# Weight conversion in an attention and MoE kernel: a sign joined from two inputs, or written as two 16-bit halves

## The chip, the cores and the metric

The kernel runs on one core of a Trainium2 chip. A core has five engines that run side by side, each with its own queue of instructions that it takes strictly in order: TensorE (PE, with its weight load PEld), VectorE (DVE), ScalarE (ACT), GpSimd (POOL) and SyncE (SP), which here issues every DMA. Results go from engine to engine through the on-chip memory SBUF and, out of TensorE, through PSUM. The metric is the time of one execution on the device, in microseconds, as the median of the runs.

## The reference: what is computed

```python
q_d = q.reshape(B, H, Sd, factor, D).mean(axis=3)     # factor 4; k_d, v_d likewise
out_up = np.repeat(sm_attn(q_d, k_d, v_d), factor, axis=2)
mask = np.abs(pos[:, None] - pos[None, :]) < factor
scores = np.where(mask, scale * (q @ k.T), -1e9)
out_local = softmax(scores) @ v
x = (out_up + out_local)      # 8 batches x 576 tokens, 512 wide
h = x @ w_in                  # 512 x 2048
g = np.maximum(0.01 * h, h)
out = g @ w_out               # 2048 x 512
```

Attention has 8 batches, 8 heads, 576 positions and a head width of 64. Its two parts, one over positions averaged by four and one over a band of seven positions, are added. Then come two dense layers over 4608 tokens. The weights w_in and w_out arrive as float64, the rest as float32.

## The kernel before

**Weights.** TensorE multiplies float32 in a rounded format (float32r). To keep precision the kernel splits every weight into a rounded part (tiles wih, woh) and the remainder (wil, wol), does the same with the activations (xh, xl; gh, gl), and adds three products for each block: high by high, high by low, low by high (L638 for the first layer, L678 for the second).

The weights must first be made from float64. One tile is 128 x 512 numbers; there are 16 of w_in and 16 of w_out, so `convert(f, k)` runs 32 times. A float64 lies in memory as two 32-bit words, the low word first. The tile `st` is seen as words: `low` is every other word from the first, `top` every other from the second. The steps are:

1. SP loads the tile (helper `load`, L181) into a staging buffer. There are seven of these, lent by other uses of the same memory: k, v, two of prod, up and, for the first few, xh1 and xl1. In the profile the tiles have these names.
2. ACT (L226) turns the low word into an integer from 0 to 7: the three bits that a float32 keeps of it, rounded. It is written over the low word.
3. DVE (L228) takes the sign bit of the top word and joins it into that integer. This is a scalar_tensor_tensor with two inputs, top and low.
4. ACT (L231) takes the absolute value of the top word, read as float32, and scales it by 2 to the power -112, so that its exponent is that of a float32.
5. DVE (L233) shifts the top word left by 3 and joins the integer of step 3 into it: now it is the float32.
6. ACT (L239) rounds it into wih or woh.
7. POOL (L241) subtracts the rounded part and writes the remainder into wil or wol. Then the staging buffer is free for another load.

**Attention.** Batch 0 is done by TensorE in bands of 64 positions (`banded`: scores L405 and L413, softmax, transposes L440, values L458 with windows of v that are loaded as su_vw). Its averaged part is `pooled` (averages by POOL L293, L295 or DVE L299, scores L312, softmax, transposes L351, values L363). The other batches' bands are done by POOL (products L507, L562) and DVE (sums L513, L568).

**Passes.** The dense layers run over half batches of 256 or 320 tokens. The first two half batches go twice, over the first eight blocks of the inner width and later over the other eight; all others go once over the 16 blocks.

**The order.** Nothing is scheduled by the compiler. Every piece of work is a generator that yields its operations with an estimated length; the class `Order` plays them through, takes at each step the operation that can start first (then the one of lower rank), and writes the instructions out in that order. An operation on an engine is estimated at a fixed part plus a part per element: on ACT 0.13 + 0.00083 n us, on DVE 0.08 + 0.00104 n, on POOL 0.25 + 0.00217 n. SP's loads are put in order in the same way, and each has to wait on the chip until the buffer that it fills is really free. So an estimate decides the place of an instruction, not when it runs.

Of the kernel before, what the change touches and what calls it, by code (L numbers as in the profile page):

```python
# [7 lines left out]
F32R = mybir.dt.float32r  # L8
I32 = mybir.dt.int32
U32 = mybir.dt.uint32  # L10
BF16 = mybir.dt.bfloat16
AF = mybir.ActivationFunctionType
ALU = mybir.AluOpType
# [21 lines left out]
LOW, ROUND = 0.876 * 2.0 ** -29, 0.484375  # L35
# [109 lines left out]
def attn_moe(ctx: ExitStack, tc, qkt, vd, qb, kb, vb0, vb1, vwb, band, identb, w_in, w_out, ident, edge, out):  # L145
    nc = tc.nc
# [11 lines left out]
    def slot(*tags):  # L158
        return (yield ("slot", tags, 0))

    def sb(s, shape, dtype, pool=None):
        tag = s.tag
        return (pool or wk).tile(shape, dtype, name=tag, tag=tag, bufs=bufs[tag])
# [4 lines left out]
    def op(eng, n, *after, times=1):  # L168
        if eng == "PE":
            dur = n  # L170
        else:
            a, k = COST[eng]
            dur = times * a + k * n
        return (yield ("op", eng, dur, max((0.0,) + after), 0, after))
# [4 lines left out]
    def load(out, in_, size, *after):  # L179
        t = yield ("op", "SP", 0.3, max((0.0,) + after), size)  # L180
        nc.sync.dma_start(out=out, in_=in_)  # L181
        return t

    def wait(name, n=1):
        return (yield ("wait", name, n))

    id_sb = const.tile([128, 128], F32, name="id_sb")
    edge_sb = const.tile([128, BLK, W], F32, name="edge_sb")
    band_sb = const.tile([128, S // 64, WIN], BF16, name="band_sb")
    idb_sb = const.tile([128, 128], BF16, name="idb_sb")  # L190
    w_in_v = w_in.rearrange("(c p) (f m) -> p f c m", p=128, m=128 * WORDS)
# [18 lines left out]
    def weight(f, k):  # L210
        f0, *ts = max((w for w in wts if w[0] <= f), key=lambda w: w[0])
        return ts[2 * k][:, f - f0], ts[2 * k + 1][:, f - f0]
# [3 lines left out]
    def convert(f, k):  # L216
        s = yield from slot("k", "v", "prod", "up", *(("xh1", "xl1") if f < 4 else ()))
        st = sb(s, [128, 512, 2], U32)
        if k == 0:
            t = yield from load(st.rearrange("p (c m) w -> p c (m w)", c=NC), w_in_v[:, f], 524e3, s.t)  # L220
        else:
            t = yield from load(st.rearrange("p m w -> p (m w)"), w_out_v[:, f], 524e3, s.t)
        low, top = st[:, :, 0], st[:, :, 1]
        li, ti, tf = low.bitcast(I32), top.bitcast(I32), top.bitcast(F32)
        t = yield from op("ACT", 512, t)
        nc.scalar.activation(out=li, in_=low, func=AF.Copy, scale=LOW, bias=ROUND)  # L226
        t1 = yield from op("DVE", 870, t)
        nc.vector.scalar_tensor_tensor(out=li, in0=ti, scalar=-(1 << 31), in1=li,  # L228
                                       op0=ALU.bitwise_and, op1=ALU.bitwise_or)
        t = yield from op("ACT", 512, t1)  # L230
        nc.scalar.activation(out=tf, in_=tf, func=AF.Abs, scale=REBIAS)  # L231
        t = yield from op("DVE", 870, t)
        nc.vector.scalar_tensor_tensor(out=ti, in0=ti, scalar=3, in1=li,  # L233
                                       op0=ALU.logical_shift_left, op1=ALU.bitwise_or)
        if f >= FSPLIT:
            yield from wait("late")
        hi, lo = (w.rearrange("p c m -> p (c m)") for w in weight(f, k))
        t = yield from op("ACT", 512, t)
        nc.scalar.copy(out=hi, in_=tf)  # L239
        t = yield from op("POOL", 590, t)  # L240
        nc.gpsimd.tensor_tensor(out=lo, in0=tf, in1=hi.bitcast(F32), op=ALU.subtract)  # L241
        s.free(t)
        od.signal(("w", f, k), t)
# [486 lines left out]
    with tc.manual_schedule():  # L730
        od.spawn(0, fixed())
        for b in range(B):
            od.spawn(0, outd_tile(b))
            for hf in range(2):
                od.spawn(0, x_tile(b, hf))
        for c in range(NC):
            od.spawn(1 + c, pooled(0, c, 1 + c, sup))
            od.spawn(1.5 + c, banded(0, c, 0, 1.5 + c, sup))
            od.spawn(26 + 0.1 * c, banded(0, c, 1, 26, sup))
        for f in range(NF):  # L740
            for k in range(2):
                od.spawn((20 if f < HF else 40) + 2 * (f % HF) + k, convert(f, k))
        od.spawn(0, swap())
        od.spawn(0, edges())
        od.spawn(0, opened())
        od.spawn(5000, down_proj())
        od.spawn(4999, up_proj())
        for b in range(BANDED, B):
            for c in range(NC):
                od.spawn(88 + 10 * b + 0.1 * c, pooled(b, c, 0))  # L750
            for hf in range(2):
                for u in range(2):
                    od.spawn(89 + 10 * b + 4 * hf + u, scores(b, hf, u))
                    od.spawn(90 + 10 * b + 4 * hf + u, widen(b, hf, u))
                    od.spawn(90 + 10 * b + 4 * hf + u, values(b, hf, u))
        od.run()
# [60 lines left out]
```

## Time and profile before

| | |
|---|---|
| median of 3 runs | 983.59 us (982.6 to 985.67) |
| the profiled execution, its own time | 980.87 us |
| its span in the profile | 979.1 us |
| mean granted clock of TensorE | 0.983 |
| joins of step 3 (L228) | 32, from 19.9 to 129.3 us of the span |
| first large matmul (L638) | 48.48 us |

The span runs from the first to the last instruction of the trace; the execution's own time has 1.77 us beside it. In the profile L228 is line 228 of the kernel, and 128x512 int32 an operand's partitions, elements and type. "Busy" counts the time from the start to the end of an instruction, so time that it spends held up after it has begun counts too. In lines of groups, idle time stands with the instruction that ended it. Three numbers with slashes are the shortest, the median and the longest duration in ns.

### The profile page before, as it was taken

To read this page: it belongs to the slowest core of one execution; us is meant where nothing else is said; L and a number is where in the kernel's file an instruction comes from. 1 tells how busy PE (TensorE), PEld (TensorE's weight loads), DVE (VectorE), ACT (ScalarE), POOL (GpSimd) and SP (SyncE) were. 2 spreads that over 40 slices of the span, in tenths; PEclk is the share of its full clock that TensorE was granted. 3 is DMA by queue.
4 is the path that set the end of the run, shared out by engine and by line. 5 is a ranking of instruction groups with operands and counts; after the bars stand their busy time and mean duration, and the time that the engine had idled before them with its cause. 6 is when DMAs were issued, how large, how long until landed. Compare 5 with 4: busy or idle time off the path is not lost.

```text
span 979.1 us, 18709 instructions
## 1 busy us (share of the span) xinstructions
PE 948.0 (97%) x7434; PEld 913.0 (93%) x7434; DVE 616.5 (63%) x987; ACT 432.2 (44%) x1251; POOL 613.5 (63%) x362
## 2 busy tenths in 40 slices
PE   5796999999999999999999999999999999999998
PEld 4596999889999999999999999999999999999998
DVE  4997778878866877587665976547563756151111
ACT  4887966444533543255422554234332324242212
POOL 3553467888797878887787878758695777310000
PEclk9597999999999999999999999999999999999999
DMA  9546763624531542225223441304131121000000
GB/s 286 188 148 204 232 223 127 197 99 156 166 108 56 185 136 94 68 92 179 82 89 109 154 147 61 111 4 158 39 108 55 54 71 52 30 23 6 23 1 27
DMA packets 51959, 106.46 MB, mean 109 GB/s; under 512 B 4464, under 2 KB 30320, under 8 KB 51872
## 3 DMA queue, kind: packets, MB, share of 16 engines
q1 hardware_dynamic: 51872, 105.28, 32.9%
q8 instruction: 58, 0.95, 0.4%
q14 instruction: 29, 0.24, 0.1%
HBM read 94.64 MB, written 10.62 MB: 108 GB/s over the span
## 4 chain that ended last, share of the span: by engine, by line
PE 91%; DMA 3%; ACT 2%; issue 1%; DVE 1%; POOL 1%; SPq 0%; POOLq 0%; ACTq 0%
PE hp L638 42%; PE acc L678 40%; PE pt L312 2%; PE pt L363 2%; PE pt L351 2%; DMA su_vw<-in_vwb_dram 1%; PE pt L598 1%; DMA v<-in_w_out_dram 1%; DMA vs<-in_vd_dram 1%; POOL wol L241 0%; POOL wil L241 0%; DVE prod L228 0%; PE pt L413 0%; ACT pd L324 0%; SPq L181 0%
## 5 line engine op out<-in xcount | busy, mean ns | idle before, releaser
L562 POOL TENSOR_TENSOR prod<-v,s 128x896 f32<-128x896 f32 (+1 forms) x112 | 270.1, 2417 | 85.8 <-DVE xloc L568 64.3
L638 PE MATMUL hp<-xh,wih 128*128 128x320 f32 (+1 forms) x1024 | 312.7, 305 | 1.7 <-ACT xh L611 1.3
L678 PE MATMUL acc<-gh,woh 128*128 128x320 f32 (+1 forms) x1024 | 307.9, 301 | 0.5 <-ACT o L713 0.4
L638 PE MATMUL hp<-xl,wih 128*128 128x320 f32 (+1 forms) x1024 | 304.0, 297 | 0.1
L638 PE MATMUL hp<-xh,wil 128*128 128x320 f32 (+1 forms) x1024 | 303.8, 297 | 0.0
L678 PE MATMUL acc<-gh,wol 128*128 128x320 f32 (+1 forms) x1024 | 301.8, 295 | 0.0
L678 PE MATMUL acc<-gl,woh 128*128 128x320 f32 (+1 forms) x1024 | 301.7, 295 | 0.0
L507 POOL TENSOR_TENSOR prod<-q,k 128x896 f32<-128x896 f32 (+1 forms) x112 | 265.1, 2373 | 36.1 <-DMA k<-in_kb_dram 22.9
L648 ACT ACTIVATE gh<-hp 128x320 fp32r<-128x320 f32 (+1 forms) x256 | 105.4, 412 | 364.5 <-PE acc L678 339.6
L651 DVE TENSOR_TENSOR gl<-hp,gh 128x320 fp32r<-128x320 f32 (+1 forms) x256 | 116.2, 455 | 221.4 <-ACT hp L649 220.3
L638 PEld LDWEIGHTS hp<-xh,wih 128*128 128x128 f32 x1024 | 194.6, 190 | 8.6 <-issue 5.5
L678 PEld LDWEIGHTS acc<-gh,woh 128*128 128x128 f32 x1024 | 192.7, 188 | 4.7 <-issue 2.6
L638 PEld LDWEIGHTS hp<-xl,wih 128*128 128x128 f32 x1024 | 195.0, 190 | 0.3 <-DVE xl L613 0.3
L638 PEld LDWEIGHTS hp<-xh,wil 128*128 128x128 f32 x1024 | 194.8, 190 | 0.0
L678 PEld LDWEIGHTS acc<-gl,woh 128*128 128x128 f32 x1024 | 192.7, 188 | 0.0
L678 PEld LDWEIGHTS acc<-gh,wol 128*128 128x128 f32 x1024 | 192.4, 188 | 0.0
L568 DVE TENSOR_REDUCE xloc<-prod 128x128 f32<-128x896 f32 (+1 forms) x112 | 133.9, 1196 | 22.7 <-POOL prod L562 21.4
L513 DVE TENSOR_REDUCE s<-prod 128x14 f32<-128x896 f32 (+1 forms) x112 | 133.4, 1193 | 19.5 <-POOL prod L507 19.1
L649 ACT ACTIVATE hp<-hp 128x320 f32<-128x320 f32 (+1 forms) x256 | 104.0, 406 | 0.0
L605 DVE TENSOR_TENSOR pt<-pt,up 128x256 f32<-128x256 f32 (+1 forms) x56 | 38.7, 709 | 32.3 <-PE pt L598 30.6
L299 DVE TENSOR_REDUCE qk_d<-qk 128x288 f32<-128x1152 f32 x29 | 38.9, 1342 | 11.8 <-DMA qk<-in_qkt_dram 11.7
L324 ACT ACTIVATE pd<-pt,st_d 128x144 f32<-128x144 f32 x84 | 32.0, 381 | 26.8 <-DVE st_d L321 19.5
(119 smaller groups left out, 777.5 us busy)
## 6 DMA issues: line engine op xcount, KB each, us to landing
qk<-in_qkt_dram SPq DMA_DIRECT2D x32, 576.0 KB
k<-in_kb_dram SPq DMA_DIRECT2D x14, 704.0 KB
v<-in_vb_dram SPq DMA_DIRECT2D x14, 704.0 KB
vs<-in_vd_dram SPq DMA_DIRECT2D x32, 288.0 KB
k<-in_kb_dram SPq DMA_DIRECT2D x14, 640.0 KB
v<-in_vb_dram SPq DMA_DIRECT2D x14, 640.0 KB
out_dram<-o SPq DMA_DIRECT2D x36, 160.0 KB
out_dram<-o SPq DMA_DIRECT2D x36, 128.0 KB
```

The lines of the kernel that those rows point to most:

```text
L299: nc.vector.tensor_reduce(out=qk_d, in_=qkr, axis=AX.X, op=ALU.add)
L324: nc.scalar.activation(out=pd[:, qi], in_=scv[:, qi], func=AF.Exp, scale=SCALE / (FAC * FAC), bias=mx[:, qi:qi + 1], accum_out=sm[:, qi:qi ...
L507: nc.gpsimd.tensor_tensor(out=prv, in0=q[:, p, a - j0:z - j0].unsqueeze(2).to_broadcast([128, n, W, D]), in1=view(k[:, p], (a - j0) * D, [ ...
L513: nc.vector.tensor_reduce(out=s[:, p, a - j0:z - j0], in_=prv, axis=AX.X, op=ALU.add)
L562: nc.gpsimd.tensor_tensor(out=prv, in0=view(v[:, p], a - j0, [[1, n], [nv, D], [1, W]]), in1=s[:, p, a - j0:z - j0].unsqueeze(2).to_broadc ...
L568: nc.vector.tensor_reduce(out=xl_t[:, :n, p], in_=prv, axis=AX.X, op=ALU.add)
L605: nc.vector.tensor_tensor(out=xv, in0=xv, in1=upv, op=ALU.add)
L638: nc.tensor.matmul(hp[:, :n], wt[:, c], x[:, c], start=k == 0, stop=k == 3 * NC - 1)
L648: nc.scalar.activation(out=gh[:, :n], in_=hp[:, :n], func=AF.Prelu, alpha=0.01)
L649: nc.scalar.activation(out=hp[:, :n], in_=hp[:, :n], func=AF.Prelu, alpha=0.01)
L651: nc.vector.tensor_tensor(out=gl[:, :n], in0=hp[:, :n], in1=gh[:, :n].bitcast(F32), op=ALU.subtract)
L678: nc.tensor.matmul(acc[:, :n], wt[:, es], g[:, :n], start=f == f0 and j == 0, stop=f == f1 - 1 and j == 2)
```

## The change

The low word, the top word and the float64 are now also seen as 16-bit halves: of the four halves of a number, 0 and 1 are the low word and 3 is the upper half of the top word, which has the sign. ACT writes its integer into half 0 alone. DVE reads half 3, keeps its highest bit and writes that into half 1, by a tensor_scalar with one input. Halves 0 and 1 together are then the word that the join made, and step 5 reads it as before. The estimate for the DVE step goes from 870 to 520 elements.

```diff
+U16 = mybir.dt.uint16
...
         low, top = st[:, :, 0], st[:, :, 1]
+        half = st.rearrange("p m w -> p (m w)").bitcast(U16).rearrange("p (m h) -> p m h", h=4)
         li, ti, tf = low.bitcast(I32), top.bitcast(I32), top.bitcast(F32)
         t = yield from op("ACT", 512, t)
-        nc.scalar.activation(out=li, in_=low, func=AF.Copy, scale=LOW, bias=ROUND)
-        t1 = yield from op("DVE", 870, t)
-        nc.vector.scalar_tensor_tensor(out=li, in0=ti, scalar=-(1 << 31), in1=li,
-                                       op0=ALU.bitwise_and, op1=ALU.bitwise_or)
+        nc.scalar.activation(out=half[:, :, 0], in_=low, func=AF.Copy, scale=LOW, bias=ROUND)
+        t1 = yield from op("DVE", 520, t)
+        nc.vector.tensor_scalar(out=half[:, :, 1], in0=half[:, :, 3], scalar1=0x8000, scalar2=None, op0=ALU.bitwise_and)
```

## The prediction

> **What bounds the kernel now.** I read the page first, for the share of each engine and for the course of the span in 40 slices.
>
> ```profile
> span 979.1 us, 18709 instructions
> PE 948.0 (97%) x7434; PEld 913.0 (93%) x7434; DVE 616.5 (63%) x987; ACT 432.2 (44%) x1251; POOL 613.5 (63%) x362
> ...
> PE   5796999999999999999999999999999999999998
> ...
> PEclk9597999999999999999999999999999999999999
> ```
>
> TensorE is busy for 97%, and what it lacks lies almost all in the first four slices of 24.5 us. So I cut the span into stages, busy time of each engine by stage.
>
> ```profile
> core 0: us, PE busy (x) PEld busy (x) DVE busy (x) ACT busy (x) POOL busy (x), PEclk, DMA share, GB/s
> 0.00:25.00 25.00, 15.09 (x118) 10.29 (x118) 12.09 (x27) 11.67 (x36) 8.96 (x15) 1.00 0.96 287
> 25.00:48.50 23.50, 17.28 (x179) 12.08 (x177) 22.05 (x35) 20.61 (x51) 12.13 (x11) 0.58 0.59 188
> 48.50:75.00 26.50, 26.29 (x270) 24.80 (x269) 24.64 (x47) 22.57 (x57) 14.44 (x11) 0.99 0.49 156
> 75.00:93.00 18.00, 10.27 (x107) 8.48 (x107) 13.79 (x23) 13.19 (x36) 4.91 (x4) 0.83 0.79 247
> 93.00:135.00 42.00, 42.00 (x310) 39.60 (x311) 32.03 (x49) 36.36 (x89) 22.14 (x15) 0.95 0.64 208
> 135.00:979.00 844.00, 837.03 (x6461) 817.73 (x6459) 511.88 (x809) 327.79 (x988) 550.95 (x308) 1.00 0.28 92
> ```
>
> ```profile
> 48.48 0.58 PE L638 MATMUL hp<-xh,wih 128*128 128x256 f32 x1
> ```
>
> Three things stand here. From 135 us on TensorE lacks 844.00 - 837.03 = 6.97 us of 844: the conversions are over, and only a changed order can act there. Between 25 and 48.5 us, before the first large matmul (the row at 48.48), DVE is busy for 94% and ACT for 88%, TensorE waits, at a granted clock of 0.58. Between 75 and 93 us TensorE lacks 18.00 - 10.27 = 7.73 us, at a clock of 0.83. A saving is worth something only where it shortens one of these two stretches; from 93 to 135 us TensorE has no gap, so what is won before is carried on.
>
> What ends the waits, by the list of waits and the chain that ended last:
>
> ```profile
> PE pt L458 <- DMA su_vw<-in_vwb_dram: 5.3, 2, 3.7
> ...
> SPq L181 <- POOL wil L241: 41.9, 13, 9.3
> ...
> 37.73 1.31 POOL wol L241
> ...
> 39.49 4.29 DMA su_vw<-in_vwb_dram
> ...
> 73.37 5.75 DMA su_vw<-in_vwb_dram
> ...
> 85.51 3.93 DMA su_vw<-in_vwb_dram
> ```
>
> Batch 0's banded values (L458) wait for small window loads. These stand in SP's one queue behind weight loads, and a weight load waits until POOL's subtraction (L241) has freed its staging buffer. So the speed of the whole conversion, ACT, DVE, ACT, DVE, ACT, POOL, sets when the windows arrive.
>
> **The join as it runs.** The operation that is replaced, by stage:
>
> ```profile
> core 0: us, DVE busy (x), PEclk, DMA share, GB/s
> 0.00:25.00 25.00, 1.38 (x2) 1.00 0.96 287
> 25.00:48.50 23.50, 7.03 (x7) 0.58 0.59 188
> 48.50:75.00 26.50, 7.59 (x7) 0.99 0.49 156
> 75.00:93.00 18.00, 4.59 (x6) 0.83 0.79 247
> 93.00:135.00 42.00, 8.92 (x10) 0.95 0.64 208
> ```
>
> That is 32 joins and 29.51 us, 0.92 each. Undisturbed one takes 0.68. The rest is seen in the timeline, where the join meets POOL's subtraction:
>
> ```profile
> 28.62 1.30 POOL L241 TENSOR_TENSOR wol<-v,woh 128x512 fp32r<-128x512 f32 x1
> ...
> 28.72 1.75 DVE L228 SCALAR_TENSOR_TENSOR prod<-prod 128x512 int32<-128x512 int32 x1
> ...
> 30.50 0.69 ACT L231 ACTIVATE prod<-prod 128x512 f32<-128x512 f32 x1 [0.39 <-DVE prod L228]
> ...
> 64.04 1.73 POOL L241 TENSOR_TENSOR wil<-k,wih 128x512 fp32r<-128x512 f32 x1 [1.32 <-ACT wih L239]
> ...
> 64.72 1.60 DVE L228 SCALAR_TENSOR_TENSOR prod<-prod 128x512 int32<-128x512 int32 x1
> 66.24 0.51 DVE L420 TENSOR_REDUCE lst<-pt 128x5 f32<-128x350 f32 x1
> ...
> 81.67 1.30 POOL L241 TENSOR_TENSOR wil<-up,wih 128x512 fp32r<-128x512 f32 x1 [2.71 <-ACT wih L239]
> ...
> 82.36 1.16 DVE L228 SCALAR_TENSOR_TENSOR prod<-prod 128x512 int32<-128x512 int32 x1
> ...
> 83.44 1.34 DVE L299 TENSOR_REDUCE qk_d<-qk 128x288 f32<-128x1152 f32 x1
> ```
>
> POOL ends at 29.92, 65.77 and 82.97; the joins end at 30.47, 66.32 and 83.52: each time 0.55 later. A join that begins while the subtraction runs stands still until it is over and then does its whole work.
>
> **The new DVE operation.** It has one input. These rows bound it:
>
> ```profile
> L228 DVE SCALAR_TENSOR_TENSOR k<-k x6: 669/684/1040, 19.9 to 115.9; 128x512 int32<-128x512 int32 x6
> ...
> L299 DVE TENSOR_REDUCE qk_d<-qk x29: 1300/1342/1353, 4.8 to 666.3; 128x288 f32<-128x1152 f32 x29
> ...
> L341 DVE TENSOR_REDUCE v_d<-vs x32: 1184/1206/1218, 14.4 to 672.3; 72x256 f32<-72x1024 f32 x32
> ...
> L321 DVE TENSOR_SCALAR st_d<-pt x28: 160/160/161, 70.7 to 670.2; 128x3 f32<-128x3 f32 x28
> ```
>
> From 1024 to 1152 elements the one-input reductions grow by 136 ns, 1.06 ns an element; 512 elements would be 1206 - 512 x 1.06 = 663 ns. The floor is 0.16 us, the same kind of operation on three elements; the ceiling is the 1.75 us of the worst join. I take 0.66, the row nearest in size and in number of inputs. The reductions matter for a second reason: 29 of them lie between 1.300 and 1.353 us although POOL is busy beside many (that at 83.44 among them). One input from SBUF was never held up by POOL here. So I expect 0.66 without the stretch: 0.92 - 0.66 = 0.26 us saved for each of 32, 8.3 us of DVE.
>
> The Trainium skill ("SBUF — State Buffer", Who interferes with whom) explains the 0.55: an operation of VectorE with two SBUF inputs and one of GpSimd exclude each other for their whole length, and this trace agrees. The same section speaks against the change, though: a tensor_scalar may enter a mode that uses both port pairs, and then it shuts GpSimd out too. "VectorE: DVE Perf Modes" (What auto-detection actually checks) has two elements a cycle for one SBUF source and destination of even length. By that the operation would take, as an estimate, 0.16 + 256/0.96 ns = 0.43 us and be blocked as before; no row here shows it.
>
> **On the path.** Three of the stretched joins lie where the chain runs. At 28.72, 1.09 us go, but ACT stood idle behind it for only 0.39: -0.4, and ACT (88% busy there) is late next. At 64.72 the reduction behind it moves from 66.24 to 64.72 + 0.66 = 65.38, and with it the second join L233, ACT's rounding, POOL's subtraction and the two weight loads that stand ahead of the window load of 73.37: -0.8. At 82.36, 0.50 go before the pooling at 83.44, which releases the matmuls ahead of the window load of 85.51: -0.5. The other joins of these stages lie beside ACT's three passes a tile, which are not shortened; if that cover were gone they would be worth 7.03 + 7.59 + 4.59 - 20 x 0.66 = 6.0 us together. Sum -1.7, with 0 and -6.0 as its ends.
>
> **ACT's 16-bit output.** The first pass writes two bytes of each eight, where it wrote four.
>
> ```profile
> L226 ACT ACTIVATE prod<-prod x12: 662/694/757, 28.0 to 121.7; 128x512 int32<-128x512 uint32 x12
> ...
> L239 ACT CAST wih<-prod x6: 647/667/753, 34.2 to 128.0; 128x512 fp32r<-128x512 f32 x6
> ```
>
> A dense output of another type is 27 ns cheaper than the stepped one, so type and step hardly count: I take 0.69, with 0.67 below and 0.76, the longest, above; 20 x 0.07 = 1.4 us of ACT before 93 us at worst, and ACT is not idle there. The wait between the two engines stays: DVE writes the upper half of the word that ACT still reads. No DMA, buffer or slot is added.
>
> **The planned order.** The diff also tells the kernel's own planner that this step takes 0.62 us (0.08 + 0.00104 x 520) in place of 0.98. All queues are written out by those times, so every engine's order may shift, SP's too. This I can't work out; it makes the rivals.
>
> The profiled execution took 980.87 us, 1.77 beside its span, 2.72 below the median of 983.59. 980.87 - 1.7 = 979.2; at the median 981.9. That is my forecast, with 980.2 to 983.5 as its own range.
>
> **Rivals.**
> 1. *All of it arrives.* The freed DVE time reaches TensorE because DVE, 94% busy, and not ACT is the limit in 25 to 48.5 us, and because less lateness there shortens the gap of 7.73 us behind. For it: DVE's share, above ACT's in both stages. Against it: ACT's idle time behind the joins. 983.6 - 6.0 = 977.6; with the whole gap of 7.73 us closed, 975.9.
> 2. *A weight load is planned ahead of a window load.* The planner now believes that a staging buffer comes free 0.36 us sooner, and SP issues in order: a weight load put one place forward holds all behind it until POOL has really freed the buffer. The wait of SP on L241 goes up to 9.3 us already, and a window load takes 3.93 to 5.75 us to land. At the price of one such landing: 983.6 - 1.7 + 5.75 = 987.6. It decides as soon as the slip exceeds 1.7 us, and is slower to be seen from 4.7 us on. Against it: the buffer in question must be one that is late, and 32 loads have 7 buffers.
> 3. *The change doesn't do what it says: it still meets POOL.* The new operation waits for the subtraction as the join does, and only the work after it is shorter, by something between 0 and 0.55 - 0.16 = 0.39 us; 0.2 at each of the three places is -0.6: 983.0. For it: every stretched join; against it: the unstretched reductions. The rule on tensor_scalar from the two pages above would give this case.
> 4. *Hidden anyway.* ACT's pass grows by its 0.07 us or sets the pace alone: 983.6.
>
> **How the numbers follow.** A measurement of this kernel tells about 0.3%, 2.95 us, from no change. Forecast 0.36 (0.08 of it beyond 2.95 us on the fast side, 0.01 on the slow), rival 1 0.28, rival 2 0.20, rival 3 0.12, rival 4 0.04. Faster 0.08 + 0.28 = 0.36; slower 0.20 + 0.01 = 0.21; same 0.43. The range of 976.0 to 988.0 reaches to rival 1 with the gap nearly closed and over rival 2 at its usual price; I leave out 0.08 for a worse slip and 0.07 for a better order.
>
> **What would show it.** In the profile after: the groups on L228 with 0.66 us and a maximum near their median (right), near 0.43 (a faster mode), or maxima of over 1 us that end a fixed time behind POOL (rival 3). L226 at 0.67 to 0.76. The first matmul of L638 some 0.4 us before 48.48 or, for rival 1, several. The missing TensorE time in the stage that now ends at 93 us below 7.73 us; above it, with L458 waiting longer for its windows, rival 2. The forecast is wrong in its reason if the time moves by more than 3 us with TensorE's waits before 93 us unchanged, that is by order after 135 us.

## The result and the profile after

| | before | after |
|---|---|---|
| median | 983.88 us | 997.72 us |
| ratio, 95% interval | | 1.0145 (1.0119 to 1.017) |
| profiled execution, its span | 980.87, 979.1 us | 997.32, 995.5 us |
| first large matmul (L638, now L639) | 48.48 us | 58.61 us |

The changed kernel is slower by 13.8 us, 1.4%. The forecast was 981.9 us, in a range of 976.0 to 988.0. One run further below, the new order with the old operations, has one execution of four left out, since it took 1043.49 us at a granted clock of 0.841 where the other three had 0.967 to 0.991; with it that run's median would be 992.92 us. Two lines were added above ACT's first pass and one taken away behind it, so ACT's first pass is now L228, VectorE's step L230, and everything behind them one line higher than before.

The same view by stage as in the prediction, of the kernel after:

```profile
core 0: us, PE busy (x) PEld busy (x) DVE busy (x) ACT busy (x) POOL busy (x), PEclk, DMA share, GB/s
0.00:25.00 25.00, 13.46 (x96) 9.16 (x97) 11.11 (x24) 10.61 (x28) 8.57 (x14) 1.00 0.96 274
25.00:48.50 23.50, 16.55 (x130) 11.18 (x129) 17.55 (x34) 23.25 (x51) 11.50 (x10) 1.00 0.61 188
48.50:75.00 26.50, 21.15 (x210) 19.20 (x210) 22.50 (x37) 23.11 (x50) 14.45 (x12) 1.00 0.41 124
75.00:93.00 18.00, 15.43 (x177) 13.91 (x172) 14.16 (x26) 17.76 (x35) 5.60 (x5) 1.00 0.73 233
93.00:135.00 42.00, 35.10 (x264) 30.49 (x262) 28.87 (x47) 35.70 (x83) 13.05 (x11) 0.88 0.59 183
```

From 25 to 48.5 us it is now ACT that has no gap: 23.25 of 23.50 us, where it had 20.61. DVE has fallen from 22.05 to 17.55, not because its step is shorter but because it is fed later: 4.5 us of its waits in this stretch are for ACT, where the kernel before has 0.3. The two operations themselves, shortest, median and longest in ns:

```profile
L228 ACT ACTIVATE k<-k x6: 1343/1371/1380, 20.2 to 125.9; 128x512 uint16<-128x512 uint32 x6
...
L230 DVE TENSOR_SCALAR prod<-prod x12: 725/778/1841, 26.7 to 138.4; 128x512 uint16<-128x512 uint16 x12
...
L230 DVE TENSOR_SCALAR k<-k x6: 742/753/825, 21.6 to 127.3; 128x512 uint16<-128x512 uint16 x6
```

ACT's pass took 669 ns on the same tiles before; it takes twice that. VectorE's one-input step, 0.75 us in the middle, is longer than the undisturbed join (0.68 us), and its maximum of 1.84 us shows that it is still held up. In the timeline:

```profile
50.20 1.56 POOL L242 TENSOR_TENSOR wil<-xl,wih 128x512 fp32r<-128x512 f32 x1 [1.35 <-ACT wih L240]
50.53 1.84 DVE L230 TENSOR_SCALAR prod<-prod 128x512 uint16<-128x512 uint16 x1
...
59.91 1.32 POOL L242 TENSOR_TENSOR wil<-prod,wih 128x512 fp32r<-128x512 f32 x1 [1.51 <-ACT wih L240]
60.13 1.71 DVE L230 TENSOR_SCALAR up<-up 128x512 uint16<-128x512 uint16 x1
```

POOL ends at 51.76 and 61.23, the steps at 52.37 and 61.84: both times 0.61 us later, as the joins ended 0.55 us later. It is the same standstill. Neither needs its whole time behind POOL's end: about 0.13 us of the undisturbed 0.68 or 0.73 is missing in both.

A measure that the granted clock doesn't disturb is how many matmuls are done by a given time. By 135 us, of the kernel before and then of the one after (the number behind PE's busy time):

```profile
0.00:135.00 135.00, 110.92 (x976) 95.25 (x977) 104.60 (x179) 104.39 (x264) 62.59 (x55) 0.89 0.68 214
135.00:200.00 65.00, 61.46 (x487) 57.22 (x486) 53.36 (x93) 34.44 (x114) 48.06 (x30) 1.00 0.57 184
200.00:250.00 50.00, 50.00 (x428) 47.68 (x427) 40.11 (x62) 23.23 (x78) 41.43 (x23) 0.97 0.38 127
```

```profile
0.00:135.00 135.00, 101.70 (x860) 83.94 (x860) 94.19 (x165) 110.43 (x242) 53.15 (x50) 0.96 0.65 196
135.00:200.00 65.00, 64.76 (x529) 60.62 (x530) 54.72 (x89) 41.74 (x127) 48.45 (x29) 1.00 0.62 189
200.00:250.00 50.00, 44.47 (x353) 42.45 (x351) 35.86 (x56) 16.68 (x51) 40.61 (x23) 0.93 0.36 116
```

TensorE is 976 - 860 = 116 matmuls behind. At 948.0 us for 7434 of them, 0.1275 us each, that is 14.8 us; it is an estimate, since matmuls differ in length. From 135 to 200 us it does 529 - 487 = 42 more than before, since it has fewer gaps there (64.76 us busy, where it had 61.46). From 200 to 250 us it does 428 - 353 = 75 fewer, in a new gap of 50.00 - 44.47 = 5.5 us. At 250 us it is thus 149 behind, 19.0 us by the same price, where the spans differ by 16.4 us.

### The profile page after: what moved, and what is told of

The parts are those of the page before. It is cut to its first block, busy times and chain, and to the rows that moved or that the text cites. A ratio compares the mean times of both kernels' runs of the same rounds, so it can differ in the third digit from the quotient of the medians.

```text
span 995.5 us, 18712 instructions
## 1 busy us (share of the span) xinstructions
PE 952.8 (96%) x7434; PEld 915.8 (92%) x7434; DVE 614.7 (62%) x987; ACT 448.2 (45%) x1251; POOL 613.0 (62%) x362
## 4 chain that ended last, share of the span: by engine, by line
PE 86%; ACT 7%; DMA 3%; DVE 2%; issue 1%; POOL 1%; SPq 0%; ACTq 0%; POOLq 0%
PE hp L639 39%; PE acc L679 39%; PE pt L313 2%; DMA k<-in_w_in_dram 2%; PE pt L352 2%; PE pt L364 2%; PE pt L599 1%; ACT prod L228 1%; ACT v L228 1%; ACT k L228 1%; POOL prod L563 1%; DVE prod L230 0%; ACT hp L650 0%; ACT prod L232 0%; DMA v<-in_vb_dram 0%
## 5 line engine op out<-in xcount | busy, mean ns | idle before, releaser
L639 PE MATMUL hp<-xh,wih 128*128 128x320 f32 (+1 forms) x1024 | 312.1, 305 | 2.2 <-DVE gl L652 2.0
L639 PE MATMUL hp<-xl,wih 128*128 128x320 f32 (+1 forms) x1024 | 303.7, 297 | 0.0
L639 PE MATMUL hp<-xh,wil 128*128 128x320 f32 (+1 forms) x1024 | 303.4, 296 | 0.0
L639 PEld LDWEIGHTS hp<-xh,wih 128*128 128x128 f32 x1024 | 194.6, 190 | 8.5 <-DVE gl L652 4.0
L639 PEld LDWEIGHTS hp<-xl,wih 128*128 128x128 f32 x1024 | 194.7, 190 | 0.2 <-DVE xl L614 0.2
L639 PEld LDWEIGHTS hp<-xh,wil 128*128 128x128 f32 x1024 | 194.5, 190 | 0.0
L612 ACT CAST xh<-pt 128x256 fp32r<-128x256 f32 (+1 forms) x56 | 22.5, 403 | 60.2 <-DVE pt L606 59.9
```

The lines of the kernel that those rows point to most:

```text
L639: nc.tensor.matmul(hp[:, :n], wt[:, c], x[:, c], start=k == 0, stop=k == 3 * NC - 1)
```

## The experiments

The change has three parts: ACT's 16-bit output, VectorE's one input with 16-bit output, and the estimate of 520, which orders all queues anew. The first four runs take them apart. A cut of code whose removed lines have 520 or write `half[:, :, 0]` is against the changed kernel, every other against the kernel before.

### Both operations, the old order

```diff
-        t1 = yield from op("DVE", 520, t)
+        t1 = yield from op("DVE", 870, t)
```

> Both new operations, but with the old estimate of 870 for the VectorE step, so that all instructions stand in the order of the kernel before. Theory A (ScalarE: the pass with 16-bit output takes 1.37 us in place of 0.69, 32 x 0.68 = 22 us more on an engine that is 99% busy from 25 to 48.5 us): the loss of 13.8 us stays, 994 to 1001 us, and L228 takes 1.37 us. Theory B (order: the estimate of 520 made a worse order): the loss goes, 983 to 987 us, though L228 takes 1.37 us. Theory C (VectorE: the one-input operation takes 0.75 us and still waits for GpSimd): the loss stays here too.

991.75 us, ratio 1.0072 (1.0057 to 1.0087). Neither theory alone: about half the loss stays with the operations, the other half goes with the order.

### The new order, the old operations

```diff
-        t1 = yield from op("DVE", 870, t)
+        t1 = yield from op("DVE", 520, t)
```

> The operations of the kernel before, ordered with the estimate of 520. Theory A: 981 to 987 us, since nothing on ScalarE is longer. Theory B: 994 to 1001 us. Theory C: as A.

992.26 us, ratio 1.0078 (1.0056 to 1.01). The estimate alone costs as much as the operations. 1.0072 x 1.0078 = 1.0151, beside 1.0145 for the whole change: within the intervals the two add up.

### VectorE's half alone

```diff
-        nc.scalar.activation(out=half[:, :, 0], in_=low, ...)
-        t1 = yield from op("DVE", 520, t)
+        nc.scalar.activation(out=li, in_=low, ...)
+        t1 = yield from op("DVE", 870, t)
```

> ScalarE writes its 32-bit integer as before; VectorE writes the sign into the upper 16 bits with one input. Order of the kernel before. The result is the same as the reference's. Theory A: 983 to 987 us (0.07 us more for each of 32 on VectorE, 2 us at most). Theory B: the same. Theory C: 994 to 1001 us.

981.98 us, ratio 0.9983 (0.9971 to 0.9996). Theory C falls. VectorE spends more on the step than before, as its busy time on that line shows, 32.31 us for 32 where the joins took 29.51:

```profile
0.00:135.00 135.00, 32.31 (x32) 0.87 0.70 214
```

It costs nothing all the same; a gain this small, with more work, is below what I could explain.

### ACT's half alone

```diff
-        nc.scalar.activation(out=li, in_=low, ...)
+        nc.scalar.activation(out=half[:, :, 0], in_=low, ...)
...
-        nc.vector.scalar_tensor_tensor(out=li, in0=ti, scalar=-(1 << 31), in1=li, and, or)
+        nc.vector.scalar_tensor_tensor(out=li, in0=li, scalar=7, in1=ti, and, and)
```

> ScalarE writes 16 bits as in the changed kernel; VectorE keeps an operation with two 32-bit inputs as before, but masks with 7 and with the top word, so the weights lose their sign and low bits (the upper half of the low word would be left uncleared otherwise). Order of the kernel before. Theory A: 994 to 1001 us. Theories B and C: 983 to 987 us.

In this kernel the weights lose their sign and low bits, so only its time is of use: 991.56 us, ratio 1.0074 (1.0058 to 1.009). This is the whole of what both operations cost in the old order. By 135 us it has done 900 matmuls:

```profile
0.00:135.00 135.00, 107.45 (x900) 89.65 (x901) 97.12 (x168) 112.77 (x247) 55.20 (x51) 0.96 0.65 196
```

ACT's busy time rises by 112.77 - 104.39 = 8.4 us while it gets through 17 instructions fewer (264 before, 247 here): the longer passes don't fit into the time that ACT had left, and what is queued behind them slides.

### What makes the 16-bit pass long

> Only a probe: the conversion's operations three times each on tiles of 128x512, attention and the dense layers are left out. ScalarE: 32-bit words at a step of two words; 16-bit halves at a step of four halves; 16-bit halves at a step of two; 16-bit dense; 32-bit dense. VectorE: the join; sign by one input into 16-bit halves; the same into a dense 16-bit tile; one input in 32-bit words stepped; one input, dense 32-bit output. The VectorE series runs once alone and once beside subtractions on GpSimd. If the 16-bit type as such costs ScalarE the double, the dense 16-bit output takes 1.37 us too; if it is that each half is written into a word or line of its own, the dense one takes 0.67 and the stepped ones 1.37. On VectorE, if one input is enough to go free of GpSimd, no one-input form is stretched beside it; if the form is what counts (two elements a cycle through both port pairs), the 32-bit one-input forms take about 0.43 us alone and are held up beside GpSimd.

Groups of the probe, ACT first, then single VectorE operations in order of time. L169 writes 32-bit words at a step of 8 bytes, L171 16-bit halves at 8 bytes, L173 halves at 4 bytes, L175 16 bits dense, L177 32 bits dense:

```profile
L171 ACT ACTIVATE sa<-src 128x512 uint16<-128x512 uint32 x3 | 4.0, 1340 | 0.0
...
L173 ACT ACTIVATE p<-src 128x512 uint16<-128x512 uint32 x3 | 2.3, 770 | 2.6 <-DMA src<-in_w_in_dram 2.6
L177 ACT ACTIVATE d<-src 128x512 int32<-128x512 uint32 x3 | 2.0, 680 | 0.1
L175 ACT ACTIVATE d<-src 128x512 uint16<-128x512 uint32 x3 | 2.0, 678 | 0.0
L169 ACT ACTIVATE sa<-src 128x512 int32<-128x512 uint32 x3 | 1.9, 648 | 0.7 <-DMA sa<-in_w_in_dram 0.7
```

Neither the type (678 dense) nor the step (648 with 32-bit words) makes it long; 16 bits written at a step of 8 bytes do: 1340 ns. The VectorE operations ran in another order than they are written; those that began before 13.32 us ran alone, those from 17.07 us on beside POOL's row of subtractions. L183 is the join, L185 halves into halves, L187 halves into a dense tile, L189 and L191 one input of 32 bits into words at a step of 8 bytes and into a dense tile:

```profile
10.13 0.42 DVE L187 TENSOR_SCALAR e<-sd 128x512 uint16<-128x512 uint16 x1
10.46 0.73 DVE L185 TENSOR_SCALAR sd<-sd 128x512 uint16<-128x512 uint16 x1
10.99 0.46 DVE L191 TENSOR_SCALAR e<-sd 128x512 int32<-128x512 int32 x1
...
13.15 0.42 DVE L189 TENSOR_SCALAR sd<-sd 128x512 int32<-128x512 int32 x1
13.32 3.67 POOL L194 TENSOR_TENSOR pd<-e,sp 128x512 f32<-128x512 f32 x1 [12.88 <-DVE e L191]
13.48 0.43 DVE L187 TENSOR_SCALAR e<-sd 128x512 uint16<-128x512 uint16 x1
...
15.16 0.69 DVE L183 SCALAR_TENSOR_TENSOR sd<-sd 128x512 int32<-128x512 int32 x1
...
17.07 28.78 POOL L196 TENSOR_TENSOR pd<-sp 128x512 f32<-128x512 f32 x24
17.37 1.53 DVE L183 SCALAR_TENSOR_TENSOR sd<-sd 128x512 int32<-128x512 int32 x1
18.82 1.26 DVE L191 TENSOR_SCALAR e<-sd 128x512 int32<-128x512 int32 x1
```

With one input and a dense output, or one in 32-bit words, the operation takes 0.42 to 0.47 us; with the halved output it takes 0.73. And beside POOL the one-input form is held up like the join (0.46 to 1.26 us). By the Trainium skill ("VectorE: DVE Perf Modes", What auto-detection actually checks) one input can run at two elements a cycle; my estimate from that page was 0.43, and the trace agrees for every output but the halved one. The Trainium skill ("SBUF — State Buffer", Who interferes with whom) has tensor_scalar contend with GpSimd in that mode, and the trace agrees here too.

It goes the other way as well. A single subtraction of POOL (L194) began at 13.32 us, while VectorE's operations followed each other without a gap up to 15.85. It took 3.67 us, where the later ones (L196) take 1.12 on average; the operations of VectorE beside it kept their 0.43 and 0.69 us.

### Where the new order loses: SP's queue and the others

SP in the old order, and in the new one with the old operations (issue start, duration, what is loaded):

```profile
36.26 0.33 SPq L181 DMA_DIRECT2D prod<-in_w_out_dram  x1
36.65 0.42 SPq L181 DMA_DIRECT2D su_vw<-in_vwb_dram  x1
39.06 0.38 SPq L181 DMA_DIRECT2D prod<-in_w_in_dram  x1
39.49 0.49 SPq L181 DMA_DIRECT2D su_vw<-in_vwb_dram  x1
42.49 0.33 SPq L181 DMA_DIRECT2D up<-in_w_out_dram  x1
```

```profile
36.62 0.33 SPq L181 DMA_DIRECT2D prod<-in_w_out_dram  x1
42.78 0.38 SPq L181 DMA_DIRECT2D prod<-in_w_in_dram  x1
43.22 0.49 SPq L181 DMA_DIRECT2D su_vw<-in_vwb_dram  x1
45.14 0.34 SPq L181 DMA_DIRECT2D up<-in_w_out_dram  x1
45.52 0.41 SPq L181 DMA_DIRECT2D su_vw<-in_vwb_dram  x1
```

The weight loads stand one place further forward, and the two windows come 6.6 and 6.0 us later. That is the move that rival 2 names. To price it, the next kernel keeps the estimate of 520 and the order of every other engine and lets a window go ahead of the weight load directly in front of it:

```diff
         t = yield ("op", "SP", 0.3, max((0.0,) + after), size)
-        nc.sync.dma_start(out=out, in_=in_)
+        if kind != "window":
+            flush()                      # issues the load that is held
+        if kind == "weight":
+            held.append((out, in_))
+        else:
+            nc.sync.dma_start(out=out, in_=in_)
```

> The operations of the kernel before, ordered with the estimate of 520, as in e2_plan_only (992.9 us), with one difference: on SP a window load of batch 0 goes ahead of the weight load that stands directly in front of it. PE, DVE, ACT and POOL keep their order instruction by instruction. Theory D (the window loads behind weight loads that wait for a staging buffer make the loss of the plan): the two windows that were issued at 43.2 and 45.5 us come some 6 us earlier, the first large matmul moves from 57.8 to about 52 us, and the time falls to 984 to 988 us. Theory E (the other queues' order makes it, above all 11 joins in place of 9 ahead of the first large matmul): 990 to 994 us.

990.05 us, ratio 1.0059 (1.0032 to 1.0086). The windows came at 35.59 and 41.84 us, the second still 2.4 us later than in the kernel before, but the first large matmul only moved from 57.78 to 56.37. The gain is 2.2 us of 8.0 by the medians, and the intervals overlap, so it isn't clear of noise. TensorE's own waits from 40 us to the first large matmul say why it is small (in brackets, the idle time and what ended it). In the kernel before:

```profile
40.81 1.07 PE L440 MATMUL pt<-id_sb,xloc 128*70 128x128 f32 x4 [2.84 <-POOL xloc L432]
...
43.91 1.12 PE L458 MATMUL acc<-su_pt,su_vw 70*64 70x64 f32 x16 [0.98 <-DMA su_vw<-in_vwb_dram]
```

In the new order with the old operations:

```profile
46.23 1.07 PE L440 MATMUL pt<-id_sb,xloc 128*70 128x128 f32 x4 [4.31 <-POOL xloc L432]
47.55 1.12 PE L458 MATMUL acc<-su_pt,su_vw 70*64 70x64 f32 x16 [0.26 <-DMA su_vw<-in_vwb_dram]
50.44 1.12 PE L458 MATMUL acc<-su_pt,su_vw 70*64 70x64 f32 x16 [1.76 <-DMA su_vw<-in_vwb_dram]
54.46 1.71 PE L312 MATMUL pt<-qk_d 64*64 64x144 f32 x12 [2.90 <-DVE qk_d L299]
```

With the windows first, where the lines are 13 higher:

```profile
44.84 1.07 PE L453 MATMUL pt<-id_sb,xloc 128*70 128x128 f32 x4 [4.34 <-POOL xloc L445]
...
53.08 1.70 PE L325 MATMUL pt<-qk_d 64*64 64x144 f32 x12 [3.79 <-DVE qk_d L312]
```

Windows that are issued 6 us later cost TensorE 2.0 us of waiting for them, only 1.0 more than before. It is itself held up longer, by the bands' softmax on POOL and by averaged scores (L312), which now stand ahead of the first large matmul and wait for DVE. With the windows first the wait for them is gone, and the wait for the averages grows from 2.90 to 3.79 us. So most of the price must lie in the other queues, as theory E had it. Another piece of it can be named. TensorE's longest wait behind 135 us, in the new order with the old operations:

```profile
208.82 0.66 PE L598 MATMUL pt<-id_sb,xloc 128*128 128x128 f32 x2 [5.49 <-DVE xloc L568]
```

Transposes stand there in PE's queue, and the sums that they need come from DVE 5.5 us after TensorE is ready. The kernel after has the same wait (5.48 us), no run with 870 has a wait of that length there (3.2 us at most). Whether matmuls behind the transposes could have run, and whether the wait would go with a later place in the queue, I have not tried.

### Is a shorter estimate worse as such?

```diff
-        t1 = yield from op("DVE", 870, t)
+        t1 = yield from op("DVE", 700, t)      # and 1040 in the second run
```

> The operations of the kernel before with an estimate of 700 for the join (0.81 us; it takes 0.92 on average, 0.68 undisturbed). Theory F (a shorter estimate is worse step by step, since the planner then puts conversions too early): between 984 and 993 us, nearer to 988. Theory G (each estimate draws another order, good or bad): anywhere from 979 to 995 us.

> The same with an estimate of 1040 (1.16 us, above the mean of 0.92). Theory F: 980 to 985 us, no worse than before. Theory G: anywhere from 979 to 995 us.

700 gives 987.2 us (ratio 1.0017, 0.9992 to 1.0042), 1040 gives 989.34 (1.005, 1.0026 to 1.0073). 700 can't be told from 870, and 1040 is slower, where theory F expected no loss: theory F falls for the larger estimate. That each estimate draws another order, good or bad (theory G), fits all four values, which lie within about 8 us, but theory G rules out little.

### Does a planner that knows the prices help?

```diff
-        t = yield from op("ACT", 512, t)
+        t = yield from op("ACT", 1500, t)
...
-        t1 = yield from op("DVE", 520, t)
+        t1 = yield from op("DVE", 870, t)
```

> The operations of the changed kernel, planned with what they take: 1.38 us for ScalarE's 16-bit pass (estimate of 1500 in place of 512) and 0.98 for VectorE's step (870). Theory A (the 22 us of ScalarE themselves make the loss of about 7 us that e1 and e4 show): 988 to 995 us, whatever the planner knows. Theory H (the loss comes from an order that was made for shorter passes): 982 to 987 us.

990.91 us, ratio 1.0085 (1.0067 to 1.0102). No: 22 us more on ACT cost 7 to 8 us in both plans tried, the one made for shorter passes and this one, which is theory A.

### Taking the window waits away

```diff
+        if b == 0:
+            s_vw = yield from slot("su_vw")
...
+            tv = yield from load(vw[:, :nb], vwb[b, c, :, b0:b1], ...)   # ahead of the scores
```

> The operations and the estimate (870) of the kernel before, but batch 0's window loads are asked for at the start of each band, ahead of the scores, and not behind the transposes. The waits of the values (L458) for su_vw, 5.3 and 1.0 us, should be gone. If these waits cost what they show: 978 to 982 us. If the planner's order matters more than any one wait: anywhere from 979 to 995 us, since all queues are ordered anew.

> As e10_windows_at_start, with VectorE's half of the change (one input, 16-bit output; ScalarE with 32-bit output). By e3 (982.0 beside 984.3 us) VectorE's half is worth 0 to 3 us: 0 to 3 us below e10_windows_at_start.

983.41 us (1.0005, 0.9992 to 1.0017), and with VectorE's half 985.48 (1.0013, 0.9996 to 1.0029): no difference from the kernel before, and none of the 0 to 3 us that VectorE's half was expected to bring. The first large matmul does start at 45.02 us, 3.5 us sooner, and the waits on su_vw are gone, but the lead is given back:

```profile
0.00:135.00 135.00, 118.53 (x998) 103.77 (x999) 102.32 (x170) 100.42 (x249) 63.77 (x55) 0.87 0.67 207
135.00:200.00 65.00, 57.39 (x430) 51.90 (x429) 53.37 (x90) 32.60 (x109) 49.38 (x31) 0.90 0.55 178
```

22 matmuls ahead at 135 us, an estimated 2.8 us at the price above; then TensorE lacks 65.00 - 57.39 = 7.6 us up to 200 us, where it lacked 3.5. Its waits there are for DVE and ACT results of batch 1. Since VectorE's half brought nothing here, the 0.17% above is not to be built on. No version was faster than the kernel before by more than that.

## Why the prediction was wrong, step by step

Two steps failed: ACT's longer pass was priced at nothing, and so was the planned order. Each alone makes about half of the 13.8 us.

- **What bounds the kernel: right in part.** ACT's 88% beside DVE's 94% was quoted and then used only as cover ("ACT (88% busy there) is late next"); an engine with 12% left was about to get longer passes. The two stretches named are not where most of the loss shows. From 25 to 48.5 us TensorE now lacks 6.95 us (6.22 before), from 75 to 93 us 2.57 (7.73 before). The new gaps are 5.35 us between 48.5 and 75 us (0.21 before) and 6.90 between 93 and 135 us (none before). The sign set for the forecast, less than 7.73 us missing in the stage up to 93 us, came all the same: the work has moved some 10 us back, and the stages no longer hold the same parts of it.
- **ACT's 16-bit output: wrong, and the first step that failed.** I took 0.69 us, from a dense and a stepped output, both of 32 bits, and concluded that "type and step hardly count". Each alone doesn't; together they do, 1.37 us. 43.09 us for the 32 passes, where the 32-bit pass takes 21.63 (in the run with VectorE's half alone); worth 7.3 us of time (ACT's half alone). The bound was drawn from rows that had none with 16 bits at a wide step.
- **The new DVE operation: wrong.** 0.66 us without the stretch was forecast; it is 0.75 undisturbed, and with the stretch 0.92 on average (29.46 us for 32), as the join was. The evidence was the reductions, one input but another operation. Rival 3, at 0.12, was right that the step still meets POOL, but not that the work behind POOL's end gets shorter (0.61 us, the join 0.55). The rule on tensor_scalar that the prediction quotes from the Trainium skill ("SBUF — State Buffer", Who interferes with whom) was borne out in the same way. The time of that part alone (0.9983) lies near the -1.7 us forecast for it, by no merit of the working: the eight microseconds of DVE that were to be saved are not, the 32 steps take 29.51 before, 29.46 in the changed kernel and 32.31 where the half stands alone.
- **On the path: not borne out.** The sum of -0.4, -0.8 and -0.5 rested on shorter steps that never came, and the runs with the windows at the start show that a lead can be given back between 135 and 200 us. "What is won before is carried on" was argued from a stage without gaps and stopped too soon.
- **The planned order: the second step that failed.** In the sum it stood at nothing, because it could not be worked out; measured alone it costs 8.0 us. Rival 2, at 0.20, named a move that did happen: a weight load went ahead of the windows, and they came 6.6 and 6.0 us later. That its price of 5.75 us is near this delay is chance, since TensorE's wait for the windows grew by only 1.0 us, and undoing the move gave back about 2 us, not clear of noise. I had priced one wait and not the other queues, where TensorE waits for POOL and DVE ahead of the first large matmul, and for 5.5 us at 209 us, beyond the stages that I looked at. How the 8.0 us divide among these waits stays open.
- **The range** ended at rival 2's price, with the forecast's own gain taken off. The two causes came together, each worth some 7 to 8 us, and the range held them neither singly nor added.

## What to carry to other kernels

Before an output is narrowed, price the combination of type and step on each engine that writes it, not the type and the step apart; a write of half words at a step of 8 bytes cost both engines more than the full word did. Where an estimate feeds a planner, time the estimate alone first: here it was worth as much as the operations, and of the three others tried none was better. And a one-input form is no way out of the standstill beside GpSimd unless the trace shows that very operation.

## What was not expected of the hardware

- ACT writes 512 elements of 16 bits at a step of 8 bytes in 1340 ns, at 4 bytes in 770, dense in 678; 32-bit words at 8 bytes take 648.
- VectorE's tensor_scalar takes 0.42 us for 512 elements from a stepped input to a dense 16-bit output or to stepped 32-bit words, 0.46 to a dense 32-bit one, and 0.73 into 16-bit halves at a step of 8 bytes.
- That tensor_scalar, with 16-bit halves as output, waits for a GpSimd subtraction in progress and ends 0.61 us behind it, where it takes 0.73 alone, although it has one input. A reduction with one input is not held up: in the kernel before, the 29 of L299 stay between 1.300 and 1.353 us, many of them begun beside POOL.
